# Merged products of k and b with a, and a state transpose in corners, in a chunked RWKV-7 kernel followed by a gated MLP

## The chip, the cores and the metric

The kernel runs on one core of a Trainium2 chip. A core has a matrix engine (PE, whose loading of stationary operands is shown apart as PEld), a vector engine (DVE), a scalar engine (ACT), a general engine (POOL) and a queue engine (SP) that issues transfers. Each has its own queue and works through it in order; semaphores tie them together. The metric is the device time of one execution in microseconds.

## The reference

Two stages follow each other. The first is a recurrence over 768 time steps for 4 batches of 8 heads with 40 channels; the second is a small MLP with the gate h * cos(h).

```python
for t in range(S):                       # S = 768, B = 4, H = 8, D = 40
    y[:, :, t] = einsum('bhd,bhde->bhe', rt, state)
    Sa = einsum('bhde,bhe->bhd', state, at)
    state = state * wt[:, :, None, :] - einsum('bhd,bhe->bhde', Sa, bt)
    state = state + einsum('bhd,bhe->bhde', vt, kt)
x = y.transpose(0, 2, 1, 3).reshape(3072, 320)
h = x @ w_in                             # 320 x 2048
out = (h * cos(h)) @ w_out               # 2048 x 320
```

All inputs and outputs are float32.

## The kernel before

**Chunks.** Time is cut into 24 chunks of C = 32 steps. Within a chunk the recurrence is written with matrices: strictly lower triangular 32 x 32 matrices of a with b (`nt`) and of a with k (`ag`), the inverse of one plus the first, and products with the state. The partition axis of 128 holds four blocks of 32, one for each batch (`blk`), or two halves of 64 of which 40 are used, one for each head parity e (`half`). Everything is float32, and one product of `mm` (L101) appears in the trace as two MATMULs and two LDWEIGHTS. A small product occupies only the part of the 128 x 128 array that its operands' partitions name: rows from where the stationary operand lies, columns from where the output lies. This text calls such a part a position.

**The steps of one chunk.** They are functions that issue to all engines:

- `p1_w`, `p1_a`, `p1_b`, `p1_n` prepare two chunks at a time. Running products of w are transposed, 1/w is taken (L395), b/w goes to `bn_b` (L396, on POOL), a times the products of w is kept transposed as `aT`, and `p1_b` transposes b/w to `bT`. `p1_n` multiplies bT with aT: 32 products of 32 stationary columns for each chunk, which ACT copies to `nt` (L459).
- After the `p1_n` of the second pair of a group of four chunks, a list of 33 small steps (`inverse`) starts: one DVE transpose (L486), 31 pairs of DVE operations (L494, L498) and one more transpose (L502) that leaves the inverses as `rt` for the whole group. The steps of the list are handed out one for each step of the main order.
- `p2_v`, `p2_k`, `p2_g` turn v, r and k/w; `p2_g` makes 32 products of k with a and 32 of v with r in one PSUM tile named gram. DVE masks the first to `ag` (L637).
- `ch_t` turns the state, which lies in `qz`, by eight transposes of 104 x 104 (L655), copied by ACT (L659). `ch_q` multiplies r with the turned state. `ch_x` adds 32 products of `ag` with v and 32 of aT with the state. `ch_s` multiplies with the inverse `rt`. `ch_z` makes the change of the state and the output `yt`.

**The MLP** is cut into pieces: `first_a` and `first_b` make h for 512 hidden columns and 256 tokens, and `second` multiplies with w_out. In the trace these are ph and po. ACT and DVE compute the gate between them. The tokens go through DRAM once (`xd`, L776 to L788) to be regrouped as `xT`.

**The order** is written by hand. For each chunk c a list `segs` names the chunk's own steps and places M at which one piece of the MLP may stand; which list is used depends on c % 4. `later(n, f)` issues f after n more steps. A group's inverse must be out before `ch_s` of its first chunk: while it isn't, a piece with four inverse steps is put in, or an inverse step alone. PSUM tiles of the small stages come from `at`, a ring of two buffers of two banks. The order of a small stage and the next piece is also coupled: after a step marked `small`, `first_b` does its 64-row products first.

**Loads** of inputs are issued by SP (L152), four for each tensor and chunk, one for each batch. The weights are rounded early in the kernel in 20 portions (`rounded`), with scratch tiles `mant`, `expo` and `sign`.

Of the kernel before, what the change touches and what calls it, by code (L numbers as in the profile page):

```python
# [9 lines left out]
F32 = mybir.dt.float32  # L10
# [10 lines left out]
def kernel(  # L21
# [55 lines left out]
    full = [slice(DP * e, DP * e + DP) for e in range(2)]  # L77
    every = slice(0, P)

    const = ctx.enter_context(tc.tile_pool(name="const", bufs=1))  # L80
# [112 lines left out]

    su = kept("su", [P, HH, C], 1, 1.0)[0]
    for i in range(4):
        nc.gpsimd.affine_select(
            su[blk[i]], su[blk[i]], pattern=[[0, HH], [1, C]], compare_op=ALU.is_gt, fill=0.0,
            base=0, channel_multiplier=-1,
        )
# [20 lines left out]

    WID = 512
    first_done, second_done = [], []

    def rounded(m, dst, src, by, by_sb):
# [16 lines left out]
        def taken():  # L241
            hi = t["words"][:, :, 1]
            t["mant"] = sb2.tile([P, WID], I32, tag="mant", name="mant")
            t["expo"] = sb2.tile([P, WID], I32, tag="expo", name="expo")
            nc.vector.tensor_scalar(t["mant"], hi, 0xFFFFF, None, ALU.bitwise_and)  # L245
            nc.vector.tensor_scalar(
                t["expo"], hi, 20, 0x7FF, ALU.logical_shift_right, ALU.bitwise_and
            )
            nc.scalar.activation(t["expo"], t["expo"], ACTF.Relu, bias=to_bits, scale=2.0**23)
            t["sign"] = sb2.tile([P, WID], mybir.dt.bfloat16, tag="sign", name="sign")  # L250
            nc.scalar.activation(t["sign"], hi, ACTF.Sign)
# [141 lines left out]
    def over_w(c, wn):  # L393
        rw = ring.tile([P, H, D], F32, tag="rw", name="rw")
        nc.vector.reciprocal(rw, wn)  # L395
        nc.gpsimd.tensor_tensor(unpad(bn_b[c % 7]), unpad(nat["b", c]), rw, ALU.mult)  # L396
        G["rw", c] = rw

    def a_W(c, aps):
# [38 lines left out]
    def p1_n(c):  # L438
# [34 lines left out]
        elif c < 8:  # L473
            lower()
        if c % 4 == 2 and c > 2:
            inv_space()

# [114 lines left out]
    def p2_kn(c):  # L592
        nc.gpsimd.tensor_tensor(unpad(kn_b[c % 2]), nat["k", c], G["rw", c], ALU.mult)
        nc.gpsimd.tensor_copy(vvm[c % 2][:, :, C : C + D], nat["v", c])
        landed(c)
# [23 lines left out]
    def p2_g(c):  # L619
        kT, vT, aT, rT = G["kT"], G["vT"], G["aT", c], G["rT", c]  # L620
        ps = at("gram")
        for j in range(4):
            for bb in range(B):
                for e in range(2):
                    mm(
                        ps[blk[bb], e, j * C : (j + 1) * C], kT[half[e], j, blk[bb]],
                        aT[half[e], j, blk[bb]], j == 0,
                    )
        for j in range(4):
            for bb in range(B):  # L630
                for e in range(2):
                    mm(
                        ps[blk[bb], e, (4 + j) * C : (5 + j) * C], vT[half[e], j, blk[bb]],
                        rT[half[e], j, blk[bb]], False,
                    )
        ag = sb2.tile([P, H, C], F32, tag="ag", name="ag")
        nc.vector.tensor_tensor(  # L637
            ag.rearrange("p (e j) t -> p e (j t)", e=2), ps[:, :, : HH * C],
            su.rearrange("p j t -> p (j t)").unsqueeze(1).to_broadcast([P, 2, HH * C]), ALU.mult,
        )  # L640
        v1 = ps[:, :, HH * C : 2 * HH * C].rearrange("p e (j t) -> p e j t", t=C)
        nc.scalar.copy(pick(vvm[c % 2], 0, (HH * NV + N72, 2), (NV, HH), (1, C)), v1)
        nc.vector.tensor_tensor(
            pick(vvm[c % 2], N72, (HH * NV - N72, 2), (NV, HH), (1, C)), v1,
            su.unsqueeze(1).to_broadcast([P, 2, HH, C]), ALU.mult,
        )
        G["ag", c] = ag


    def ch_t(c):  # L650
        ps = at("sT")
        n = DP + D
        G["s"] = sb1.tile([P, 2 * B, n], F32, tag="s", name="s")
        for i in range(2 * B):
            nc.tensor.transpose(  # L655
                ps[:n, i // 4, (i % 4) * n : (i % 4 + 1) * n], qz[:n, i // 2, i % 2, C : C + n], ident[:n, :n]
            )
        for i in range(2):
            nc.scalar.copy(G["s"][:n, 4 * i : 4 * i + 4].rearrange("p i e -> p (i e)"), ps[:n, i, : 4 * n])  # L659

    def ch_q(c):
        ps = at("qps")
        for i in range(2 * B):
            for e in range(2):
                for f in range(2):
                    mm(
                        ps[half[e], f, i * C : (i + 1) * C], G["s"][half[f], i, half[e]],
                        G["rT", c][half[f], 2 * (i % 2) + e, blk[i // 2]], i == 0,
                    )
# [6 lines left out]
    def ch_x(c):  # L676
        ps = at("x0ps")
        for j in range(4):
            o = C * (j // 2)
            for bb in range(B):  # L680
                for e in range(2):
                    mm(
                        ps[blk[bb ^ e], e, j * N72 : (j + 1) * N72], G["ag", c][blk[bb], 4 * e + j, :],
                        vvm[c % 2][blk[bb], 2 * j + e, o : o + N72], j == 0,
                    )
        if c:
            for j in range(4):
                o = (NZ - N72) * (j // 2)
                for bb in range(B):
                    for e in range(2):  # L690
                        mm(
                            ps[blk[bb ^ e], e, j * N72 : (j + 1) * N72],
                            G["aT", c][half[e], j, blk[bb]], qz[half[e], bb, j % 2, o : o + N72], False,
# [6 lines left out]
    def ch_s(c):  # L700
        ps = at("sps")
        x0 = G["x0"]
        for j in range(4):
            for bb in range(B):
                for e in range(2):
                    g = bb ^ e
                    mm(
                        ps[blk[bb], e, j * N72 : (j + 1) * N72], G["rt", c][blk[g], 4 * e + j, :],
                        x0[e][blk[g], j * N72 : (j + 1) * N72], j == 0,
                    )  # L710
# [7 lines left out]
        for e in range(2):  # L718
            nc.vector.tensor_tensor(  # L719
                pick(sm[e], D, (2 * N72 - D, 2), (N72, 2), (1, C)),  # L720
                pick(ps[:, e], 0, (2 * N72 + D, 2), (N72, 2), (1, C)),
                su.rearrange("p (f m) t -> p f m t", f=2), ALU.mult,
            )
        G["sm"] = sm

    def ch_z(c):
# [10 lines left out]
        for s, n in ((0, kn_b[c % 2]), (1, bn_b[c % 7])):  # L737
            for j in range(4):
                o = C - C * (j // 2)
                for bb in range(B):  # L740
                    for e in range(2):
                        first = wide and not s
                        mm(
                            ps[bb // 2][(full if first else half)[e], bb % 2, j * N72 : (j + 1) * N72],
                            n[blk[bb], 2 * j + e, : DP if first else D],
                            sm[e][blk[bb], j, :] if s else vvm[c % 2][blk[bb], 2 * j + e, o : o + N72],
                            first and j == 0,
# [138 lines left out]
    def p1(c):  # L886


        def first_w():
            p1_w(c)  # L890
            if c == 4:
                later(1, lambda: load(6, "w"))

        def both_a():
            p1_a(c)
            if c == 4:
                later(1, lambda: load(7, "w"))
# [6 lines left out]

        return [first_w, both_a, lambda: p1_b(c), lambda: p1_n(c)]

# [7 lines left out]
    def p2(c):  # L914
# [4 lines left out]

        return [lambda: p2_v(c), lambda: p2_k(c), last]  # L920

# [8 lines left out]
    with tc.manual_schedule():  # L930
# [119 lines left out]
        for c in range(NCH):  # L1050
            t, q, x, s, z = main(c)
            v, k, g = p2(c + 1) if c + 1 < NCH else [lambda: None] * 3
            q0 = c - c % 4 + 4
            fill, pn, pn4 = (1, 4), None, None
            if c == 0:
# [27 lines left out]
            elif c == 5:  # L1083
                pw, pa = p1(10)[:2]
                pb, pn = p8
                segs = [t, M, pb, q, M, pn, k, M, x, M, s, S6, M, z, M, S7, M, pw, v, M, g, pa, M]
            elif c % 4 == 0 and q0 < NCH:
                pb, pn = p1(q0)[2:]
                segs = [t, v, M, q, M, k, x, M, g, M, s, pb, M, z, M, pn, M, M]
                if q0 + 4 < NCH:  # L1090
                    segs.insert(-1, lambda: scanned(c // 4 + 2))
            elif c % 4 == 1 and q0 < NCH:
                pw, pa = p1(q0 + 2)[:2]
                segs = [t, M, pw, q, M, x, k, M, s, v, M, z, M, pa, M, g, M, M]
            elif c % 4 == 2 and q0 < NCH:
                pb, pn = p1(q0 + 2)[2:]
                segs = [t, M, pb, q, M, pn, v, M, x, M, s, k, M, g, M, z, M, M]
            elif c % 4 == 3 and q0 + 4 < NCH:
                pw, pa = p1(q0 + 4)[:2]
                segs = [t, M, pw, q, M, x, k, M, s, v, M, z, M, pa, M, g, M, M]  # L1100
            else:
                segs = [t, v, M, q, M, x, k, M, g, M, s, M, M, z, M, M]
            n = len(segs)
# [9 lines left out]
            for i, seg in enumerate(segs):  # L1113
# [8 lines left out]
                if seg is not M:  # L1122
                    G["kind"] = "q" if seg is q and c > 3 else "other"
                    step(seg, *((0, 0) if c < 3 and seg in (*firsts, *seconds) else fill), small=seg in (q, x, g, s, z, pn, pn4, *firsts, *seconds))
                    if seg not in (*firsts, *seconds) and (c < 2 or c == 2 and not done):
# [7 lines left out]
                while i == n - 1 and c > 3 and done < goal and c != 4 and allowed(c):  # L1133
                    piece(*fill)
                if seg is pn and (c == 3 or c > 4 and c % 4 == 2):
                    inv_steps.extend(by_blocks(q0) if c == 3 else inverse(q0))
        for g, work, j, _ in pieces[done:]:
# [35 lines left out]
```

## Time and profile before

| what | value |
|---|---|
| median of 3 runs | 800.21 us (799.5 to 800.78) |
| the profiled execution's own time | 800.58 us |
| its span, first to last instruction | 798.9 us |
| granted PE clock, mean over the span | 0.983; 1.00 in every stretch of 10 us from 100 to 790 us |
| POOL busy | 25% of the span |
| chain that ended last: largest parts | ph 22%, po 20%, x0ps 3%, dps 3%, gram 3%, rw (1/w) 3% |
| DMA queues of the inputs | 52.11 MB, 30.6% of 16 engines' span |

The chain of work that ended last is followed back from the last instruction; a share is the part of the span for which an engine or a line was what everything else waited for. A line of the timeline gives the start in us, the length in us, the engine, the source line, output and inputs, their shapes (rows times columns of the array for PE) and how many instructions were merged. In the table of groups the number ahead of the comma is the group's busy time in us, and the one behind it the mean length of one instruction in ns.

A period of four chunks takes 116 us in the middle of the kernel (387 to 503 us). DVE's busiest stretch in it is the one of the inverse.

### The profile page before, as it was taken

The page shows a single profiled execution, that of the slowest core. Times are in us where ns is not written, and L with a number is a line of the kernel's source. Part 1 is how long each engine was busy: PE and PEld are TensorE (multiplying, and loading weights), DVE is VectorE, ACT ScalarE, POOL GpSimd, SP SyncE. Part 2 cuts the span into 40 slices and gives each one's busy share as a digit, 9 for nine tenths or more (in the row PEclk, how much of TensorE's full clock was granted, in tenths as well). Part 3 has the DMA queues.
Part 4 walks back from the last instruction along what each step waited for, and adds up shares of the span by engine and source line. Part 5 has one row for each costly group of instructions (what it writes and reads, how often), then busy time and mean ns, then how long its engine had stood idle before and what let it go on. Part 6 is the DMA issues. An engine that isn't in the chain of part 4 may idle for free.

```text
span 798.9 us, 39602 instructions
## 1 busy us (share of the span) xinstructions
PE 745.9 (93%) x17812; PEld 571.0 (71%) x17812; DVE 486.7 (61%) x1025; ACT 383.4 (48%) x723; POOL 199.9 (25%) x354
## 2 busy tenths in 40 slices
PE   4768798999999999999999999999999999999997
PEld 4535576777766777777777787777787777777775
DVE  8768858864734896554895645994346863323331
ACT  1336567564435436545535635534545445354352
POOL 5326635230321330330330230332031122201000
PEclk9888899999999999999999999999999999999999
DMA  8575563343353314334214324223220222001000
GB/s 112 150 187 140 146 152 88 60 124 64 59 122 64 67 36 65 72 99 70 60 38 66 93 43 73 46 49 68 43 46 21 46 46 55 19 18 32 20 17 16
DMA packets 183304, 55.79 MB, mean 70 GB/s; under 512 B 157152, under 2 KB 178656, under 8 KB 183136
## 3 DMA queue, kind: packets, MB, share of 16 engines
q1 hardware_dynamic: 177440, 52.11, 30.6%
q8 instruction: 140, 2.29, 1.2%
q10 hardware_dynamic: 5440, 0.82, 0.8%
q0 software_dynamic: 256, 0.33, 0.3%
q14 instruction: 28, 0.23, 0.1%
HBM read 42.07 MB, written 11.14 MB: 67 GB/s over the span
## 4 chain that ended last, share of the span: by engine, by line
PE 65%; DVE 14%; DMA 5%; ACT 5%; issue 4%; POOL 3%; SPq 2%; DVEq 0%; ACTq 0%; POOLq 0%
PE ph L101 22%; PE po L101 20%; PE x0ps L101 3%; PE dps L101 3%; PE gram L101 3%; DVE rw L395 3%; PE vT L330 2%; PE sps L101 2%; PE qps L101 2%; PE nps L101 2%; DVE inv_tmp L494 2%; DVE inv L498 2%; DVE mant L245 1%; SPq L152 1%; PE kT L330 1%
## 5 line engine op out<-in xcount | busy, mean ns | idle before, releaser
L101 PE MATMUL po<-w_out_sb,gT 128*128 128x320 f32 x768 | 223.5, 439 | 0.1
L101 PE MATMUL ph<-xT,w_in_sb 128*128 128x256 f32 x768 | 185.7, 386 | 0.1
L101 PEld LDWEIGHTS po<-w_out_sb,gT 128*128 128x128 f32 x768 | 140.2, 190 | 54.6 <-issue 2.3
L101 PEld LDWEIGHTS ph<-xT,w_in_sb 128*128 128x128 f32 x768 | 139.3, 190 | 29.7 <-issue 12.4
L830 ACT ACTIVATE turns<-ph,rnd 128x512 f32<-128x512 f32 x96 | 64.1, 685 | 156.3 <-PE ph L101 155.9
L832 DVE SCALAR_TENSOR_TENSOR turns<-turns,ph 128x512 f32<-128x512 f32 x96 | 64.0, 683 | 109.4 <-ACT turns L830 109.2
L840 DVE TENSOR_TENSOR gT<-ph,turns 128x512 f32<-128x512 f32 x96 | 65.8, 686 | 38.4 <-ACT turns L837 38.4
L756 POOL TENSOR_TENSOR qz<-qz,wc 128x160 f32<-128x160 f32 x92 | 41.9, 475 | 168.5 <-DVE qz L755 167.9
L837 ACT ACTIVATE turns<-turns,half_pi 128x512 f32<-128x512 f32 x96 | 69.3, 722 | 3.1
L836 ACT ACTIVATE turns<-turns 128x512 f32<-128x512 f32 x96 | 60.1, 626 | 19.0 <-DVE turns L832 19.0
L101 PE MATMUL ph<-xT,w_in_tail 64*128 64x256 f32 (+1 forms) x512 | 54.6, 394 | 1.6 <-issue 1.6
L498 DVE TENSOR_TENSOR inv<-inv,inv_tmp 128x31 f32<-128x31 f32 (+15 forms) x124 | 51.2, 413 | 4.3
L755 DVE TENSOR_TENSOR qz<-dps,qz 128x160 f32<-128x160 f32 x92 | 28.9, 314 | 37.6 <-PE dps L101 37.3
L586 POOL COPY vp<-nat_v 128x320 f32<-128x320 f32 x24 | 11.7, 487 | 159.9 <-DMA nat_v<-in_v_dram 139.6
L494 DVE TENSOR_TENSOR inv_tmp<-u,inv 128x31 f32<-128x31 f32 (+15 forms) x124 | 48.5, 391 | 2.3
L395 DVE RECIPROCAL rw<-nat_w 128x320 f32<-128x320 f32 x20 | 42.8, 2142 | 0.1
L101 PEld LDWEIGHTS ph<-xT,w_in_tail 64*128 64x128 f32 (+1 forms) x512 | 32.2, 160 | 10.8 <-issue 7.3
L767 POOL TENSOR_TENSOR yt<-yt,wb 128x512 f32<-128x512 f32 x24 | 31.6, 1318 | 22.1 <-DVE yt L762 22.1
L659 ACT COPY s<-sT 104x416 f32<-104x416 f32 x46 | 20.8, 503 | 33.1 <-PE sT L655 33.1
L719 DVE TENSOR_TENSOR sm<-sps,su 128x128 f32<-128x128 f32 x48 | 11.7, 285 | 33.1 <-ACT sm L714 30.3
L396 POOL TENSOR_TENSOR bn<-nat_b,rw 128x320 f32<-128x320 f32 x22 | 19.9, 905 | 44.3 <-DVE rw L395 44.2
L671 ACT COPY qz<-qps 40x512 f32<-40x512 f32 x46 | 26.6, 579 | 6.8 <-PE qps L101 6.4
(136 smaller groups left out, 1100.3 us busy)
## 6 DMA issues: line engine op xcount, KB each, us to landing
words<-in_moe_w_in_dram SPq DMA_DIRECT2D x8, 512.0 KB
xd<-yt SPq DMA_DIRECT2D x48, 80.0 KB
out_dram<-ot SPq DMA_DIRECT2D x24, 160.0 KB
nat_k<-in_k_dram SPq DMA_DIRECT2D x92, 40.0 KB
nat_v<-in_v_dram SPq DMA_DIRECT2D x92, 40.0 KB
nat_r<-in_r_dram SPq DMA_DIRECT2D x92, 40.0 KB
nat_a<-in_a_dram SPq DMA_DIRECT2D x84, 40.0 KB
ws<-in_w_dram SPq DMA_DIRECT2D x5, 640.0 KB
```

What stands on the lines that cost most here:

```text
L101: nc.tensor.matmul(o, lhsT=lhsT, rhs=rhs, start=start, stop=stop, skip_group_check=True)
L395: nc.vector.reciprocal(rw, wn)
L494: nc.vector.tensor_tensor(tmp, u[:, j : j + 1, :j].to_broadcast([P, C - j, j]), x[:, j:, j : j + 1].to_broadcast([P, C - j, j]), ALU.mult,)
L498: nc.vector.tensor_tensor(x[:, j:, :j], x[:, j:, :j], tmp, ALU.subtract)
L755: nc.vector.tensor_tensor(z, pick(dp, 0, (2 * N72 + C, 2), (N72, 2), (1, D)), z, ALU.add)
L756: nc.gpsimd.tensor_tensor(z, z, wc.rearrange("p (f m b) -> p f m b", f=2, m=2)[:, :, :, bb] .unsqueeze(3).to_broadcast([P, 2, 2, D]), ALU. ...
L767: nc.gpsimd.tensor_tensor(yt.rearrange("p j b t -> p (j b) t"), yt.rearrange("p j b t -> p (j b) t"), wx, ALU.mult)
L830: nc.scalar.activation(n, u, ACTF.Identity, bias=rnd, scale=1.0)
L832: nc.vector.scalar_tensor_tensor(n, n, -ROUND, u, ALU.add, ALU.subtract)
L836: nc.scalar.activation(n, n, ACTF.Abs)
L837: nc.scalar.activation(n, n, ACTF.Sin, bias=half_pi, scale=-2.0 * math.pi)
L840: nc.vector.tensor_tensor(gT[:, 2 * e : 2 * e + 2].rearrange("p f t -> p (f t)"), us[e], ns[e], ALU.mult)
```

## The change

From chunk QT = 8 on, k/w is also loaded and divided early (`early_k`, `early_kn`), turned together with b/w (`p1_kb`), and interleaved so that each product has 64 stationary columns, 32 of k and 32 of b. `p1_kn` multiplies these with aT: 32 products a chunk give both triangular matrices. Its output has k and b on alternating blocks, so the copies to `nt` (ACT) and the masks to `ag` (DVE) are made for each block of 32 partitions. For the result to meet its partner, the odd heads of bn, kn, v and k/w are stored with their two halves of the partition axis exchanged (`placed`: three POOL operations instead of one), and `spot` gives the block in which a product finds its operands. `p2_k` is left out from there on, and `p2_g` keeps only the products of v and r. From chunk 6 on `ch_t` turns the state by 32 products of 40 x 40 with the identity. Scratch for the weights' rounding and the new tiles share one buffer, `cv`. The lists of steps are rewritten to hold `p1_kb` and `p1_kn` of each chunk, and the inverse starts behind the fourth `p1_kn` of a group.

```diff
+    QT = 8
+
+    def spot(c, bb, e):
+        p = bb ^ 2 * e
+        return (p, p ^ 1) if c >= QT else (bb, bb ^ e)
...
+    cv = const.tile([P, 5 * WID], F32, tag="cv", name="cv")
+    kb = cv[:, : 4 * P * 2]
+    ke = cv[:, 1024:1344].rearrange("p (h d) -> p h d", d=D)
+    kne = cv[:, 1344:1856].rearrange("p (h d) -> p h d", d=DP)
...
+    def placed(c, dst, x, by=None):
+        lo, hi = slice(0, P // 2), slice(P // 2, P)
+        parts = [(every, every, slice(0, H, 2)), (lo, hi, slice(1, H, 2)), (hi, lo, slice(1, H, 2))]
+        for to, of, h in parts if c >= QT else [(every, every, slice(0, H))]:
+            if by is None:
+                nc.gpsimd.tensor_copy(dst[to, h], x[of, h])
+            else:
+                nc.gpsimd.tensor_tensor(dst[to, h], x[of, h], by[of, h], ALU.mult)
...
+    def p1_kb(c):
+        ps = at("kbT")
+        turned(ps[:, 0], kne)
+        turned(ps[:, 1], bn_b[c % 7])
+        for i, o, n in ((0, 0, 3 * C), (1, C, C)):
+            nc.scalar.copy(
+                pick(kb, o, (4 * C, 2 * B), (n, 2), (1, C)),
+                pick(ps[:, i], 0, (2 * C, 2 * B), (C, 2), (1, C)),
+            )
...
+    def p1_kn(c):
+        ps = at("nps")
+        for j in range(4):
+            for x in range(2):
+                for m in range(2):
+                    for e in range(2):
+                        p = 2 * m + x
+                        bb = p ^ 2 * e
+                        mm(
+                            ps[slice(m * DP, (m + 1) * DP), e, (4 * x + j) * C : (4 * x + j + 1) * C],
+                            pick(kb[half[e]], (j * B + p) * DP, (1, DP)), G["aT", c][half[e], j, blk[bb]],
+                            j == 0 and x == 0,
+                        )
...
+        for g in range(B):
+            for x, to, put in (
+                (1 - g % 2, G["nt"][blk[g], :, c % 4].rearrange("p t e j -> p e j t"), nc.scalar.copy),
+                (g % 2, ag[blk[g]].rearrange("p (e j) t -> p e j t", e=2), None),
+            ):
...
     def ch_t(c):
         ps = at("sT")
+        if c > 5:
+            s = sb1.tile([P, 2, 2 * B, D], F32, tag="s", name="s")
+            for i in range(2 * B):
+                for e in range(2):
+                    for f in range(2):
+                        o = C + DP * f
+                        mm(
+                            ps[half[f], e, i * D : (i + 1) * D], qz[half[e], i // 2, i % 2, o : o + D],
+                            ident[half[e], half[e]], i == 0,
+                        )
...
     def ch_x(c):
                 for e in range(2):
+                    p, g = spot(c, bb, e)
                     mm(
-                        ps[blk[bb ^ e], e, j * N72 : (j + 1) * N72], G["ag", c][blk[bb], 4 * e + j, :],
-                        vvm[c % 2][blk[bb], 2 * j + e, o : o + N72], j == 0,
+                        ps[blk[g], e, j * N72 : (j + 1) * N72], G["ag", c][blk[p], 4 * e + j, :],
+                        vvm[c % 2][blk[p], 2 * j + e, o : o + N72], j == 0,
                     )
...
     def ch_s(c):
                 for e in range(2):
-                    g = bb ^ e
+                    p, g = spot(c, bb, e)
                     mm(
-                        ps[blk[bb], e, j * N72 : (j + 1) * N72], G["rt", c][blk[g], 4 * e + j, :],
+                        ps[blk[p], e, j * N72 : (j + 1) * N72], G["rt", c][blk[g], 4 * e + j, :],
                         x0[e][blk[g], j * N72 : (j + 1) * N72], j == 0,
                     )
...
             elif c % 4 == 2 and q0 < NCH:
-                pb, pn = p1(q0 + 2)[2:]
-                segs = [t, M, pb, q, M, pn, v, M, x, M, s, k, M, g, M, z, M, M]
+                kb2, kn2, kb3, kn3 = p1(q0 + 2)[2:]
+                segs = [t, M, kb2, q, M, kn2, v, M, x, kb3, M, s, M, kn3, M, z, M, g, M]
...
-                if seg is pn and (c == 3 or c > 4 and c % 4 == 2):
-                    inv_steps.extend(by_blocks(q0) if c == 3 else inverse(q0))
+                if seg is pn and c == 3:
+                    inv_steps.extend(by_blocks(q0))
+                if c > 4 and c % 4 == 2 and kns and seg is kns[1]:
+                    inv_steps.extend(inverse(q0))
```

## The prediction

> **What bounds the kernel now.** I read the page first (busy shares, then the chain that ended last), then PE's timeline over one steady period of four chunks (420 to 536 us), then DVE's over the same stretch. The page:
>
> ```profile
> PE 745.9 (93%) x17812; PEld 571.0 (71%) x17812; DVE 486.7 (61%) x1025; ACT 383.4 (48%) x723; POOL 199.9 (25%) x354
> ...
> PE 65%; DVE 14%; DMA 5%; ACT 5%; issue 4%; POOL 3%; SPq 2%; DVEq 0%; ACTq 0%; POOLq 0%
> ```
>
> PE is busy for 93% of the span, and from chunk 8 on its timeline has almost no holes. So an edit is worth the PE time that it adds or takes. A PE stage's price is the distance from its start to the next stage's start, not its summed busy time, since small products overlap. Timeline lines (start in us, length, work):
>
> ```profile
> 182.00 0.73 PE L101 MATMUL below<-rn,noff 32*32 32x16 f32 x64
> 182.66 2.42 PE L101 MATMUL po<-w_out_sb,gT 128*128 128x320 f32 x8
> ```
> ```profile
> 421.34 0.82 PE L101 MATMUL qps<-rT,s 40*40 40x32 f32 x64
> 421.98 1.14 PE L101 MATMUL ph<-xT,w_in_tail 64*64 64x256 f32 x16
> ...
> 429.39 0.73 PE L101 MATMUL gram<-aT,kT 40*32 40x32 f32 x62
> ...
> 429.95 0.73 PE L101 MATMUL gram<-rT,vT 40*32 40x32 f32 x62
> 430.61 2.42 PE L101 MATMUL po<-w_out_sb,gT 128*128 128x320 f32 x8
> ...
> 441.05 1.29 PE L101 MATMUL nps<-aT,bT 40*32 40x32 f32 x128
> 442.27 4.57 PE L101 MATMUL po<-w_out_sb,gT 128*128 128x320 f32 x16
> 446.68 0.88 PE L655 MATMUL sT<-ident,qz 104*104 104x104 f32 x8
> 447.40 1.91 PE L101 MATMUL ph<-xT,w_in_sb 128*128 128x256 f32 x8
> ...
> 458.05 0.88 PE L101 MATMUL sps<-x,rt 32*32 32x72 f32 x64
> 458.86 0.66 PE L330 MATMUL vT<-ident,vp 128*128 128x128 f32 x4
> ```
>
> Each fp32 product is two MATMULs (32 products, x64). The reader should see that 64 MATMULs cost 0.5 to 0.8 us whatever they compute. What sets that is in the single start times. sps starts in waves of 8, 62.5 ns apart (458.183, 458.246, 458.308); gram in waves of 8 about 32 ns apart; qps in waves of 4, 38 ns apart; below in waves of 4, 32 ns apart. The code gives the number of different positions (rows of the array x columns) that each stage uses: 8, 8, 4, 4. So one MATMUL runs at each position at a time, and a wave lasts as long as the longer of two things: streaming (72 columns: 62.5 ns, 0.87 ns a column) and loading the stationary operand (below streams 16 columns, 14 ns, yet needs 32 ns for 32 stationary columns; qps needs 38 for 40). After the first 33 or so, eight-position stages pause for 65 ns and run on at 8.3 ns a MATMUL, another limit, which leaves sps at 0.66 us from first start to last.
>
> ```profile
> L101 PEld LDWEIGHTS sps<-x,rt 32*32 32x32 f32 x1536 | 17.7, 106 | 13.8 <-issue 7.5 <-DVE x L697 3.9 <-DVE gT L840 1.3
> ...
> L101 PEld LDWEIGHTS dps<-vvm,kn 32*64 32x64 f32 x1280 | 16.2, 130 | 8.8 <-issue 6.5 <-DVE turns L832 1.3 <-ACT half L556 0.5
> ```
>
> A load of 64 columns is 24 ns longer than one of 32 (106 against 130 ns in the mean column; inside the waves 105 and 131, 26 apart). So a 64-column load needs 32 + 26 = 58 ns of its position.
>
> **The change, part by part.** Around a stage of small positions PE also loses 0.09 us going in (the last po before sps is followed after 0.363 us, before sT after 0.269) and, to the next full-size stage, 0.12 us after a 32-column stream, 0.15 after 72.
>
> 1. Products of k and b with a (16 chunks, 8 to 23). Out, for four chunks: the four pairs of gram stages, 4 x (0.09 + 0.53 + 0.69) = 5.24; kT's transposes, 0.44 to 0.49 each, 1.91; nps twice, 2 x (0.09 + 1.22) = 2.62; bT twice, 0.93 and 0.87, 1.80. Together 11.57 us. In: gram with v and r alone, 4 x (0.09 + 0.56 + 0.12) = 3.08; eight transposes a chunk for k and b, 0.93 each but 0.87 ahead of qps, 3.66; 32 products a chunk of 64 stationary columns at 4 positions, 16 waves of 58 ns, first to last start 15 x 58 + 20 = 0.89, so 4 x (0.09 + 0.89 + 0.12) = 4.40. Together 11.14. A gain of 0.43 us in four chunks, 1.7 in sixteen. Halving the MATMULs here halves no time, since half the positions carry loads nearly twice as long. Bounds of the gain: 0.3 us if 64 columns load in twice the 32 ns of 32, and 6.1 us at qps's 0.62 from first to last start.
>
> 2. Positions of x0ps and sps. To make the merged output fit, `spot` sends block p = bb ^ 2e to p ^ 1 for both e. The ag products of x0ps and all of sps then use four positions (0 to 1, 1 to 0, 2 to 3, 3 to 2) instead of eight. At 62.5 ns a wave of four, 16 waves: 15 x 62.5 + 20 = 0.96 us against 0.66. That is 0.30 us, twice a chunk, 16 chunks: +9.5 us. Bounds: 0 (the positions do not bind) to 72 ns a wave as qps's surplus of 11 ns over its 27 ns stream would give, +14. dps, gram and the aT half of x0ps keep eight positions. I take 9.5; the sps row is the same product.
>
> 3. State turned by 32 products (18 chunks, 6 to 23). sT costs 0.715 now (446.68 to 447.40) as full-size work without the losses around it. As 64 MATMULs of 40 stationary and 40 moving columns at 4 positions it is qps: 0.09 + 0.62 + 0.12 = 0.83. +0.12 x 18 = +2.1 us; bounds 0 and +4 (a 72-column sps's 0.81 plus its 0.09).
>
> 4. The inverse. It begins when the last n-product of its four chunks is out. Before, that is nps early in the chunk with c % 4 = 2 (481.93); now it is the fourth product, behind s (490.31) and another piece: 10 to 12 us later. DVE's rows and its reader:
>
> ```profile
> 486.76 1.23 DVE L486 STREAM_TRANSPOSE u<-nt 128x1024 f32<-128x1024 f32 x1
> ...
> 538.28 1.97 DVE L502 STREAM_TRANSPOSE rt<-inv 128x1024 f32<-128x1024 f32 x1
> ```
> ```profile
> 548.92 1.23 PE L101 MATMUL sps<-x,rt 32*32 32x72 f32 x64
> ```
>
> rt is ready at 540.25, 8.7 us ahead of its reader, so the delay eats the margin and a little more. At one step per PE step, 31 of the 33 inverse steps come before s; the kernel then puts one more piece ahead of it (1.8 us of PE work, no loss by itself). DVE's rows between u and rt sum to about 49 us (inverse 28, the rest 21), and PE's stages from the same point to that s, at the prices above, to about 50: DVE finishes as PE arrives. I charge 0.5 us at each of four places (q0 = 8, 12, 16, 20), +2.0. Bounds: -4 (the present waits of PE in this stretch, 0.67, 0.38 and 0.76 us, go) to +16.
>
> 5. Hidden work. ACT: four nt copies of 32 partitions a chunk in place of one of 128 (two of those take 1.03 us in a row), +1.5 us a chunk, and longer s copies, +0.3: about 31 us on 383. DVE: four masks of 0.42 for one, +20 on 487. POOL: bn, kn and vvm in three parts each and k/w a second time, three rows near 0.475 (qz's 160 columns) for one of 0.905: about 2.7 us a chunk, +43 on 200. All three stay below 65%, behind pieces of 1.8 to 4.5 us; uncovered, one late copy per chunk of 0.3 us would be 5 us. SP issues 64 more loads of k, four in 1.9 to 3.1 us. Its queue passes xd and nat loads behind them; it is idle for 5 to 7 us at the end of each long burst (323 to 328), which two such groups just fill, and xT is first read about half a chunk later. The weights' rounding, whose buffers k now reuses, ends at 140 us, before the first such load. I charge nothing.
>
> Sum: +9.5 + 2.1 - 1.7 + 2.0 = +11.9 us on the profiled execution's 800.58 (span 798.9), which is 0.4 above the median of the runs (800.21). Rounded down for that: 812.
>
> **The rivals.** *Number of instructions decides* (faster). PE's stages cost by count, not position: 64 columns at qps's rate give 6.1, sps and x0ps stay, sT costs gram's 0.78, +1.2. 800.6 - 6.1 + 1.2 = 795.7. For it: all 64-MATMUL stages lie between 0.5 and 0.8 us. Against it: waves of four where four positions are used, and 32 ns for a 16-column stream. [...]
>
> *Row groups decide.* The new order walks all four row blocks in turn, where now each comes twice running. If only a row's being taken held a product up, part 2 would cost nothing: 800.6 + 2.1 - 1.7 + 2.0 = 803.0. Against it: sps has 8 in a wave on four row blocks, below 4 on the same four. [...]
>
> *DVE becomes the bound at the inverse* (slower still). If rt comes 4 us late at each of four places, 812 + 14 = 826. For it: DVE is 92 to 97% busy from 500 to 540; against it: the sum above, with the small steps last.
>
> **How the numbers follow.** The forecast has 0.60 and its own range 806 to 820 (parts 2 and 4); the late inverse 0.13 (820 to 832); row groups, or half of part 2, 0.11 (799 to 806); instruction count 0.16 (790 to 799). The range 798 to 826 leaves out most of the last and the top of the second, 0.2 together. A measurement here tells 0.2%, 1.6 us, from no change: faster 0.17, same 0.06, slower 0.77.
>
> **What would show it.** sps and the first half of x0ps at about 1.11 and 1.08 us to the next start instead of 0.81; the 64-column stage at 1.0; sT at 0.75 or more; PE holes ahead of sps at chunks 8, 12, 16, 20 below 1 us. I am wrong if sps still takes 0.81, if the merged stage takes qps's 0.64, or if PE shows new holes behind ACT, POOL or SP.

## The result, and the profile after

The change costs time: 875.1 us (872.0 to 878.4, 4 runs) beside 800.5 us for the kernel before in the same comparison, a ratio of 1.092 with a 95% interval of 1.088 to 1.095. The prediction had the sign, 812 us in place of 875, and a range that ends at 826.

The page of the kernel after the change, busy time and share by engine, then the granted PE clock in 40 slices of the span, then the chain that ended last:

```profile
span 872.2 us, 39911 instructions
...
PE 780.4 (89%) x17780; PEld 592.2 (68%) x17780; DVE 507.4 (58%) x1073; ACT 426.2 (49%) x771; POOL 256.7 (29%) x499
...
PEclk9778999999987999999999997999999999999999
...
PE 58%; DVE 15%; ACT 10%; DMA 7%; issue 4%; SPq 4%; POOL 3%; POOLq 0%; DVEq 0%; ACTq 0%
```

Three things grew. The span is 73.3 us longer (872.2 against 798.9). PE idles for 91.8 us of it (872.2 less 780.4) where it idled for 53.0: 38.8 us. The mean granted clock is 0.956 in place of 0.983; 1 - 0.956 of 872.2 is 38.4 us, against 13.6: 24.8 us. What is left is 9.7 us, and that is the only part that the prediction summed up (9.5 + 2.1 - 1.7 = 9.9). That the two agree so closely is partly luck. The split belongs to these two executions: the mean clock was 0.949 to 0.956 in the four runs of the kernel after the change and 0.966 to 0.981 in 30 runs of the kernel before beside the experiments, and by the middle of both the loss of clock is nearer 20 us than 25. In the chain, ACT's share went from 5% to 10%.

The timeline of PE in the new kernel, about one end of a chunk with c % 4 = 1 and the start of the next (start, length, work; the idle time ahead of a line and what ended it stand in brackets):

```profile
516.43 1.14 PE L107 MATMUL nps<-aT,cv 40*64 40x32 f32 x64
517.49 2.42 PE L107 MATMUL po<-w_out_sb,gT 128*128 128x320 f32 x8
519.85 0.76 PE L107 MATMUL gram<-rT,vT 40*32 40x32 f32 x64
523.03 1.30 PE L107 MATMUL sT<-ident,qz 40*40 40x40 f32 x64 [2.43 <-DVE ag L550]
524.26 3.78 PE L107 MATMUL ph<-xT,w_in_sb 128*128 128x256 f32 x8
...
534.32 0.66 PE L344 MATMUL vT<-ident,vp 128*128 128x128 f32 x4
...
539.67 2.06 PE L107 MATMUL x0ps<-vvm,cv 32*32 32x72 f32 x64 [2.10 <-DVE cv L550]
```

The merged product (nps) takes 1.06 us to the next start, close to the 1.01 of the prediction (0.89 and 0.12). But the turn of the state, which needs nothing of it, starts 2.43 us late behind the last mask of that product, and the eight MATMULs of ph behind it take 3.78 us where they take 1.99 elsewhere. At 539.67 the same again. Holes of 0.3 us or more behind the masks add up to about 26 us from 200 us on.

Why the masks hold up a stage that does not read them is seen in the same kernel's timelines of ACT and of DVE, four entries each for one merged product:

```profile
535.29 0.57 ACT L548 COPY nt<-nps 32x256 f32<-32x256 f32 x1
536.34 0.59 ACT L548 COPY nt<-nps 32x256 f32<-32x256 f32 x1 [0.48 <-DVE cv L550]
537.42 0.58 ACT L548 COPY nt<-nps 32x256 f32<-32x256 f32 x1 [0.48 <-DVE cv L550]
538.48 0.58 ACT L548 COPY nt<-nps 32x256 f32<-32x256 f32 x1 [0.49 <-DVE cv L550]
```
```profile
535.90 0.41 DVE L550 TENSOR_TENSOR cv<-nps,su 32x256 f32<-32x256 f32 x1 [1.07 <-ACT nt L548]
536.97 0.42 DVE L550 TENSOR_TENSOR cv<-nps,su 32x256 f32<-32x256 f32 x1 [0.66 <-ACT nt L548]
538.03 0.42 DVE L550 TENSOR_TENSOR cv<-nps,su 32x256 f32<-32x256 f32 x1 [0.64 <-ACT nt L548]
539.09 0.43 DVE L550 TENSOR_TENSOR cv<-nps,su 32x256 f32<-32x256 f32 x1 [0.64 <-ACT nt L548]
```

Eight operations on one PSUM tile, each waiting for the one before on the other engine, from 535.29 to 539.52: 4.2 us. The tile is one of the two buffers of `at`. The stage after next that asks for a buffer (here x0ps; vT took the other) starts at 539.67, 0.15 us behind the last mask. In all 16 of these tiles of this kernel each of the eight but the first starts 0.03 us behind the end of the one before (three times 1.01 us, where DVE had other work), also where a mask and the next copy read different blocks. Why operations on different blocks wait for each other is not shown by these traces.

### The profile page after: what moved, and what is told of

Same layout as the page of the kernel before. It is cut to its first block, busy times and chain, and to the rows that moved or that the text cites. A ratio compares the mean times of both kernels' runs of the same rounds, so it can differ in the third digit from the quotient of the medians.

```text
span 872.2 us, 39911 instructions
## 1 busy us (share of the span) xinstructions
PE 780.4 (89%) x17780; PEld 592.2 (68%) x17780; DVE 507.4 (58%) x1073; ACT 426.2 (49%) x771; POOL 256.7 (29%) x499
## 4 chain that ended last, share of the span: by engine, by line
PE 58%; DVE 15%; ACT 10%; DMA 7%; issue 4%; SPq 4%; POOL 3%; POOLq 0%; DVEq 0%; ACTq 0%
PE ph L107 20%; PE po L107 17%; PE x0ps L107 4%; PE dps L107 4%; ACT nt L548 3%; PE sps L107 3%; SPq L158 3%; PE kbT L344 2%; DVE rw L409 2%; PE vT L344 2%; PE qps L107 2%; ACT turns L944 1%; DVE cv L550 1%; PE sT L107 1%; PE nps L107 1%
## 5 line engine op out<-in xcount | busy, mean ns | idle before, releaser
L107 PE MATMUL po<-w_out_sb,gT 128*128 128x320 f32 x768 | 231.1, 448 | 0.0
L107 PE MATMUL ph<-xT,w_in_sb 128*128 128x256 f32 x768 | 191.0, 394 | 0.5 <-DMA xT<-xd 0.5
L107 PEld LDWEIGHTS po<-w_out_sb,gT 128*128 128x128 f32 x768 | 142.4, 194 | 55.5 <-issue 5.2
L107 PEld LDWEIGHTS ph<-xT,w_in_sb 128*128 128x128 f32 x768 | 142.6, 194 | 32.9 <-issue 12.3
L548 ACT COPY nt<-nps 32x256 f32<-32x256 f32 x64 | 37.6, 587 | 42.5 <-PE nps L107 16.4
L570 DVE TENSOR_TENSOR inv_tmp<-u,inv 128x31 f32<-128x31 f32 (+15 forms) x124 | 51.5, 415 | 1.9
L421 POOL TENSOR_TENSOR bn<-nat_b,rw 64x160 f32<-64x160 f32 (+2 forms) x54 | 31.4, 582 | 39.5 <-DVE rw L409 24.9
L409 DVE RECIPROCAL rw<-nat_w 128x320 f32<-128x320 f32 x20 | 42.8, 2142 | 0.0
L107 PEld LDWEIGHTS ph<-xT,w_in_tail 64*128 64x128 f32 (+1 forms) x496 | 32.3, 168 | 10.2 <-issue 6.7
L107 PEld LDWEIGHTS sps<-x,rt 32*32 32x32 f32 x1536 | 23.5, 109 | 18.1 <-issue 14.2
```

The costliest lines, as they stand in the source:

```text
L107: nc.tensor.matmul(o, lhsT=lhsT, rhs=rhs, start=start, stop=stop, skip_group_check=True)
L548: put(to, of)
L570: nc.vector.tensor_tensor(tmp, u[:, j : j + 1, :j].to_broadcast([P, C - j, j]), x[:, j:, j : j + 1].to_broadcast([P, C - j, j]), ALU.mult,)
```

## The experiments

Times in the text are medians of the runs; the last table is made from the profiled executions. The kernel before, run beside each set of experiments, had medians of 798.2 to 802.2 us, so a difference of some 4 us between kernels of different sets shows little.

**Is it the eight evacuations?** One ACT copy and one DVE mask for the whole tile; with this layout every other block then gets the other matrix.

```diff
-        for g in range(B):
-            for x, to, put in (...
+        nc.scalar.copy(G["nt"][:, :, c % 4].rearrange("p t e j -> p e j t"), of(1))
+        nc.vector.tensor_tensor(ag.rearrange("p (e j) t -> p e j t", e=2), of(0), ...)
```

> The eight evacuations behind each merged product (4 of ScalarE, 4 masks of VectorE, 4.3 us in series) become one of each over 128x256; every other row block of the stationary and of the mask output then holds the other half, so the values differ, the work on every other engine is the same. Theory (the series of eight holds one of the two PSUM buffers and makes the holes, and the holes lower the clock): the 26 us of PE holes behind the masks go, and with them about two thirds of the 25 us of lost clock: 825 to 840 us, mean granted clock 0.97 or more, no hole of 2 us behind the masks. Rival 1 (the loads and GpSimd's pieces of k in chunks 5 to 7 set the pace): 865 or more. Rival 2 (TensorE's own small products cost more than their rows show): 860 or more with no holes left.

836.5 us (835.1 to 837.9), 38.6 less. No hole is left behind the masks, and the idle time of PE falls from 91.8 to 66.0 us. Both rivals would have kept it at 860 or above. The clock only rose to 0.964, where 0.97 was expected; two low stretches stayed at 210 to 265 us, behind the holes ahead of kbT.

**The buffer, or the work?** ACT copies the whole tile to SBUF first, and the eight operations read that.

```diff
+        st = cv[:, :512].rearrange("p (e n) -> p e n", e=2)
+        nc.scalar.copy(st, ps[:, :, : 2 * HH * C])
```

> ScalarE first copies the whole PSUM result to SBUF (128x512, 0.6 us), and the four copies and four masks read that, with the same outputs as before. Work on ScalarE grows by 16 times 0.6 us, VectorE's stays. Theory (it is the PSUM buffer that is held too long): nearly all of the relief of the single pass, 828 to 845 us. Rival (it is the work of ScalarE and VectorE that is too much, whatever it holds): 870 to 890.

847.0 us (843.4 to 850.6): 28 us back with more work on ACT than before, a little above the range. In ACT's timeline of this kernel the operations no longer take turns:

```profile
394.06 0.57 ACT L542 COPY cv<-nps 128x512 f32<-128x512 f32 x1
394.66 2.57 ACT L548 COPY nt<-cv 32x256 f32<-32x256 f32 x4
```

The buffer is free after 0.57 us, and the four copies run in one piece. So most of the loss is the buffer held for 4.2 us. The other 10 us are the difference to one_pass, which has less work on both engines; part of them is seen on PE, where kbT waits for 1.35 us three times (398, 520 and 643 us) until ACT, behind its four copies, has read the turned v and r out of the other buffer. No run gives the ring a third buffer.

**The turns, or their sum?** All four copies first, then the four masks.

> The kernel after the change, with the four ScalarE copies of each merged product ahead of its four VectorE masks, where they alternated (same outputs). Theory (the sum of eight operations in series is what counts, 4 times 0.58 and 4 times 0.42 us, and seven handoffs of about 0.06 us are only a tenth of it): 866 to 876 us. Rival (the alternation is the cost): 845 to 860.

870.8 us (870.2 to 871.3). The copies run for 2.4 us, then the masks for 1.7: 4.1 us in place of 4.2, and the holes ahead of x0ps are 1.9 to 2.0 us in place of 2.1. Ahead of the turn the hole is 1.35 us in place of 2.4: there 1.2 us of DVE's work on the gate stood between the first copy and its mask and lengthened the series to 5.25 us, and with the copies first it runs beside them. PE's idle time falls by 4 us (91.8 to 87.5), the clock is no better (0.954). So it is mostly the sum that counts, and the alternation is the smaller part.

**The holes at 211 and 264 us.** In the kernel after the change, on PE:

```profile
257.25 1.99 PE L107 MATMUL ph<-xT,w_in_sb 128*128 128x256 f32 x8
264.05 1.11 PE L344 MATMUL kbT<-ident,cv 128*128 128x128 f32 x4 [4.80 <-POOL cv L421]
```

The queue of SP stood for up to 11.9 us at the load of the early k (L504), whose one buffer POOL had not read yet. First attempt: two buffers for it.

```diff
-    ke = cv[:, 1024:1344].rearrange("p (h d) -> p h d", d=D)
+    kes = [cv[:, o : o + H * D].rearrange("p (h d) -> p h d", d=D) for o in (1024, 2368)]
```

> The early k has two buffers in place of one, so that its load no longer waits for GpSimd to have read the last one. Theory: the two holes of 4.6 and 4.8 us ahead of the k and b transposes at 211 and 264 us go or shrink, and some of the low clock behind them: 858 to 868 us. Rival 1 (the masks alone count, and the loads queue behind others anyway): 871 to 877. Rival 2 (this chain is the main cause): below 850.

869.7 us (868.9 to 870.4), some 5 us less, between the ranges of the theory and of rival 1; the two holes of 4.55 and 4.80 us stood unchanged. So the buffer was not what kbT waited for there. POOL's timeline of the kernel after the change says what was:

```profile
250.28 1.69 POOL L421 TENSOR_TENSOR bn<-nat_b,rw 128x160 f32<-128x160 f32 x3 [1.18 <-DVE rw L409]
259.74 1.69 POOL L421 TENSOR_TENSOR bn<-nat_b,rw 128x160 f32<-128x160 f32 x3 [7.76 <-issue]
261.49 0.45 POOL L662 COPY vp<-nat_v 128x320 f32<-128x320 f32 x1
261.88 0.46 POOL L662 COPY rp<-nat_r 128x320 f32<-128x320 f32 x1
262.30 1.70 POOL L421 TENSOR_TENSOR cv<-cv,rw 128x160 f32<-128x160 f32 x3
```

The last line is the early k of chunk 10, which needs only the 1/w of the first line's chunk. It stands behind b/w of chunk 11, which waits for a reciprocal on DVE (L409, 257.47 to 259.61 us), and behind vp and rp; POOL is idle for 7.76 us with its work queued in the wrong order. So the early k is issued ahead of the next chunk's w and b:

```diff
         def both_a():
+            if c >= QT:
+                early_kn(c)
             p1_a(c)
-            if c >= QT:
-                later(1, lambda: early_kn(c))
```

> The single pass of the run before (one ScalarE copy and one VectorE mask per merged product, values differ), and GpSimd's three pieces of the early k of chunk c are issued ahead of the work on chunk c+1's w and b, where they stood behind it. Theory (the two holes of 4.6 and 4.8 us ahead of the k and b transposes come from GpSimd's order: the early k stands behind the products of b and 1/w of the next chunk, which wait for VectorE's reciprocal): the 9.4 us of holes and the low clock of 200 to 280 us go: 815 to 826 us. Rival (the load of k is what is late, the order is not): the holes stay, 832 to 840.

838.9 us (838.5 to 839.3): nothing gained over one_pass. Both holes ahead of kbT are gone, but five of 1.5 to 3.1 us came ahead of ph, four of them behind a transfer. So the order made the two holes, as the theory has it, and the time is still the rival's. SP's queue and PE of this kernel:

```profile
483.99 0.37 SPq L881 DMA_DIRECT2D xd<-yt  x1
488.22 1.80 SPq L504 DMA_DIRECT2D cv<-in_k_dram  x4
490.12 0.39 SPq L891 DMA_DIRECT2D xT<-xd  x1
```
```profile
494.09 3.75 PE L107 MATMUL ph<-xT,w_in_sb 128*128 128x256 f32 x8 [3.07 <-DMA xT<-xd]
```

The load of the early k now stands between the store and the read-back of x and holds SP for 4 us until POOL has read its one buffer. The staged form with the same edit shows it too:

> The staged copy (same outputs) with GpSimd's early k issued ahead in the same way. Theory: 847 less the same 11 to 20 us, 826 to 836 us, some 10 us above the single pass, which is ScalarE's extra copies and the eight small operations. Rival (ScalarE's queue is the bound in this form): 840 or more.

846.6 us (845.9 to 847.2), no gain over 847.0. With the new order it is the second buffer that was missing:

> Single pass, early k ahead on GpSimd, and two buffers for the early k (values differ by the single pass). Theory (in the run before, the load of the early k stood in SP's queue between the store and the read-back of x, waiting up to 4 us for GpSimd to have read its one buffer, and made the four new holes of 2 to 3 us ahead of the first MoE product): these holes and the low clock behind them go, 9.8 plus some 7 us: 817 to 826 us, so that the early work on k and b costs little beyond TensorE's own longer stages (10 us) and the late inverse (5 us and its clock). Rival (the time goes elsewhere each time a hole is closed, because the whole of ACT, DVE, GpSimd and SP is too full): 832 or more.

827.1 us (825.8 to 828.5), 1 us above the range: 9.4 less than one_pass. Of the holes ahead of ph one of 4.1 us is left. The staged form:

> Staged copy (same outputs), early k ahead, two buffers for the early k. Theory: the holes ahead of the first MoE product (5 us) and the low clock behind them go: 834 to 842 us. Rival (ScalarE's queue, 10 us more of copies than in the single pass, takes the gain): 844 to 850.

839.3 us (838.9 to 839.8), as expected, and the fastest form that computes all of the change: 1.045 of the time before (1.039 to 1.051), slower still.

**TensorE's own price, measured alone.** The kernel before with only the positions of x0ps and s changed (values differ):

```diff
-                        ps[blk[bb ^ e], e, j * N72 : (j + 1) * N72], G["ag", c][blk[bb], 4 * e + j, :],
-                        vvm[c % 2][blk[bb], 2 * j + e, o : o + N72], j == 0,
+                        ps[blk[g], e, j * N72 : (j + 1) * N72], G["ag", c][blk[p], 4 * e + j, :],
+                        vvm[c % 2][blk[p], 2 * j + e, o : o + N72], j == 0,
```

> The kernel before the change, with only the 32 products of ag in x0 and the 32 of s put on four array positions from chunk 8 on, as the change puts them (the operands are read from other row blocks, so the values differ). Theory: 16 chunks times twice 0.30 us, all on the path: 808 to 812 us, with s and the first half of x0 at 1.11 to 1.14 us each. Rival 1 (the row groups bound the stage, not the positions): 802 to 804. Rival 2 (the waits behind the longer stages add to it): above 814.

806.9 us, a ratio of 1.0092 (1.0056 to 1.0128) to the 798.2 us of the kernel before in this comparison: 4.5 to 10.2 us. The time is 1 us under the range, which was counted from 800 us, and above that of rival 1. PE's timeline of this kernel, against 0.81 to the next start in the kernel before:

```profile
460.24 1.20 PE L107 MATMUL sps<-x,rt 32*32 32x72 f32 x64
461.38 0.65 PE L336 MATMUL vT<-ident,vp 128*128 128x128 f32 x4
```

And the kernel before with only the turn by 32 small products:

> The kernel before the change, with only the turn of the state by 32 small products in corners from chunk 6 on (same outputs). Theory: 18 times 0.04 us on TensorE, and two ScalarE copies of 0.7 us in place of 0.46 us ahead of q, of which some 0.1 us a chunk is waited for: 1 to 4 us slower than before. Rival (the copies are waited for in full, 18 times 0.48): 8 us or more slower.

808.3 us, a ratio of 1.0067 (1.0037 to 1.0098): 3.0 to 7.9 us, more than expected. Its timeline of PE says where:

```profile
450.36 4.57 PE L101 MATMUL po<-w_out_sb,gT 128*128 128x320 f32 x16
454.87 0.83 PE L101 MATMUL sT<-ident,qz 40*40 40x40 f32 x64
455.62 1.99 PE L101 MATMUL ph<-xT,w_in_sb 128*128 128x256 f32 x8
457.45 1.04 PE L330 MATMUL wT<-ident,nat_w 128*128 128x128 f32 x8
```

Against the lines of the kernel before that the prediction shows: po to sT 4.51 us where it was 4.41 (446.68 less 442.27), sT to ph 0.75 for 0.72, and ph to the next full-size stage 1.83 us, where it took 1.75 behind the transposes. Together some 0.21 us, most of it in the two neighbours. Not every chunk is like this one: in chunks 8, 12 and 16, where transposes of v stand behind the turn, the same three distances add up to 0.01 us more, and over all 18 chunks they add up to 2.8 us, 2.4 of it in the neighbours. Where the rest of the 3.0 to 7.9 us lies stays open. In the kernel after the change the turn was undone:

> The state is turned by 8 transposes in every chunk again, as before the change; all else is as after. Theory: 18 times 0.04 us of TensorE and 18 times 0.5 us of ScalarE's copies, of which part is waited for: 868 to 874 us. Rival (the 32 products of the turn disturb TensorE's queue or the chain of the state beyond what their row shows): below 865.

872.2 us (870.9 to 873.6), 2.9 us less, which the spread of the kernel after the change (872.0 to 878.4) does not tell from nothing.

**Does the idle PE itself bring the low clock?** Dummy matmuls in the idle places of the kernel after the change, of chunks 6, 10, 14 and 18:

> The kernel after the change, with dummy matmuls (8 to 10 of 0.25 us, 5 ahead of the third place) put in TensorE's queue where it stood idle behind the masks in chunks 6, 10, 14 and 18: ahead of the turn of the state 2.4 us, ahead of the first x0 product 2.1 us, ahead of the last products 1.2 us. The waits stay as long, TensorE is only not idle in them. Theory (an idle stretch of some 2 us is followed by a lower granted clock, which costs about as much again): clock 0.97 or more and 857 to 868 us. Rival (the lower clock has another cause, or the dummies only take the place of the wait): 872 to 880.

885.0 us (884.2 to 885.7), 10 more. This did not test it: ahead of x0ps the dummies asked for a buffer of po and waited themselves (4.4 us in place of 2.1), and the ten ahead of the turn filled 1.0 of the 2.4 us. Again, with more of them and only where po's buffer is at hand:

```diff
+        FILL.update({(m, i): n for m in (10, 14, 18) for i, n in ((0, 24), (15, 12))})
```

> The kernel after the change, with 24 dummy matmuls (0.1 us each) ahead of the turn of the state and 12 ahead of the last products in chunks 10, 14 and 18, so that TensorE is not idle in the 2.4 and 1.2 us there; the waits of 2.1 us ahead of the first x0 product stay idle. Theory (the idle stretch brings the lower granted clock): no granted clock under 0.97 within 10 us behind the filled places (0.66 at 395 to 400 and 0.54 at 525 to 530 us in the kernel after), and 864 to 872 us. Rival (the waits alone and the low clock have a common cause elsewhere): the same low stretches at the same places, 873 to 878.

871.8 us (871.3 to 872.3). Stretches of 5 us of PE (from and to, length, busy time, granted clock, then the DMA share and GB/s, not used here), first of the kernel after the change, then of this one:

```profile
520.00:525.00 5.00, 2.57 (x130) 0.77 0.40 67
525.00:530.00 5.00, 5.00 (x51) 0.54 0.44 69
```
```profile
520.00:525.00 5.00, 4.66 (x157) 1.00 0.34 56
525.00:530.00 5.00, 5.00 (x99) 1.00 0.49 79
...
405.00:410.00 5.00, 3.17 (x16) 1.00 0.45 72
410.00:415.00 5.00, 4.72 (x138) 0.66 0.40 62
```

Behind all the filled places the clock stays at 1.00, also at the two (395 and 523 us) behind which it had dropped, and at 410 us it drops at an x0ps that was left idle. The turn waits as long behind gram in both kernels (3.18 us from start to start), so it is PE's idling that lowers the clock, not what made it wait. The 3.3 us that this saved are no more than the spread of the kernel after the change.

**The last 25 us.** The inverse came 3.9 us late ahead of chunk 20. Two of its steps were handed out at a time from chunk 19 on, in single_first_two:

```diff
-                segs = [t, v, M, q, M, x, M, g, M, s, M, M, z, M, M]
+                segs, fill = [t, v, M, q, M, x, M, g, M, s, M, M, z, M, M], (2, 4)
```

> Single pass, early k ahead, two buffers, and from chunk 19 on two steps of the inverse with each step of work in place of one (values differ by the single pass). Theory (the inverse of the last group came 3.9 us late because VectorE was given one step at a time and stood idle between): the hole ahead of s in chunk 20 and the low clock behind it go: 819 to 824 us. Rival (VectorE is full there and the steps only push other work back): 826 or more.

827.7 us (827.0 to 828.5): the hole is gone and nothing is gained. New ones came instead (1.0 us ahead of a turn, 1.7 us ahead of a q, behind ACT's copy of the turned state), and a low clock at 641 us, ahead of both. The same with the turn undone:

> As inverse_sooner, with the state turned by 8 transposes again. Theory (the turn costs what it cost in the kernel before, 3 to 8 us, once no hole hides it): 4 to 8 us under inverse_sooner, 812 to 818 us, and so within some 5 us of the kernel before plus the 9 us of four positions. Rival 1 (it costs the 2 to 3 us that undoing it brought in the kernel after): 817 to 822. Rival 2 (a further loss is still unnamed): 820 or more.

825.4 us (822.0 to 828.7), above both of the first two ranges and in that of rival 2, a loss still unnamed; the spread is too wide to price the turn again. What is left is seen by groups of chunks. The table is worked out from the starts of the stage sT in the profiles, in us:

| kernel | chunk 5 to 8 | 8 to 12 | 12 to 16 | 16 to 20 | 20 to end | idle PE | clock lost |
|---|---|---|---|---|---|---|---|
| before | 95.4 | 115.7 | 116.0 | 110.7 | 155.2 | 53.0 | 13.6 |
| after | 126.8 | 128.0 | 130.7 | 121.5 | 161.0 | 91.8 | 38.4 |
| one_pass | 109.3 | 121.0 | 120.2 | 115.9 | 160.7 | 66.0 | 30.1 |
| single_first_two | 100.5 | 120.5 | 120.0 | 115.0 | 161.0 | 59.1 | 23.1 |
| before_4pos | 94.1 | 117.7 | 118.2 | 112.9 | 157.7 | 48.3 | 20.2 |

Of the 73 us by which the span grew, 31 lie in chunks 5 to 8, where the masks and POOL's order meet, 11 to 15 in each of the next three groups and 6 in the last. Once those are undone (single_first_two), a group costs 4.0 to 4.8 us more than before. The four positions alone make 2.0 to 2.2 of it, and the rows of the turn, in the kernel before, 0.5 to 0.7. The small holes do not make the rest: single_first_two has 1.5 to 1.9 us of holes of 0.3 to 0.7 us in a group (0.66 ahead of the second half of x0ps, 0.43 ahead of s, 0.45 ahead of vT), and the kernel before has 1.5 and 1.8 us in other places in the first two of these groups (0.76 ahead of vT, 0.33 to 0.67 ahead of s, 0.38 ahead of the next vT), 0.8 in the third. So 1 to 2 us of a group stay without a cause. The clock column includes the first 100 us, where 13.7 to 18.8 us are lost in the kernels of the table, whatever the change.

## Why the prediction was wrong

- *Part 1, the merged products:* right as far as the rows go. The stage takes 1.06 us (1.01 predicted), kbT 0.93 and, ahead of qps, 0.97 (0.93 and 0.87), gram of v and r alone 0.69 (0.68 predicted: 0.56 between the first and the last start of gram's MATMULs in the kernel before, 429.92 to 430.49 us, and 0.12). The small gain of this part was not run alone.
- *Part 2, four positions:* right. 1.13 us to the next start for s and the first half of x0ps (1.11 and 1.08 predicted), and 4.5 to 10.2 us measured alone against 9.5. The rivals of instruction count and of row groups fall with it.
- *Part 3, the turn:* mis-sized, 2.1 us against 3.0 to 7.9. The term of 0.83 us (loss going in, stage, loss to the next) measured 0.85. What it left out is the stage behind, where ph is 0.08 us longer; but not all 18 chunks have these neighbours, and all in all the rows give 2.8. The upper bound of +4 is 3.3 by the part's own figures (0.90 less 0.715, 18 times).
- *Part 4, the inverse:* the delay was there, 0.43, 0.42, 0.44 and 3.71 us, 5.0 in all against 2.0, within its bounds. Closing the longest did not pay.
- *Part 5, the hidden work:* this is the step that failed, at "I charge nothing". It counted the busy time that the change adds to ACT, DVE and POOL and compared it with their shares (all below 65%, which still holds, though ACT grew by 43 us in place of 31 and POOL by 57 in place of 43). It did not ask what the eight evacuations hold while they run: one of two PSUM buffers for 4.2 us, sixteen times. It allowed 5 us for copies that come late; the single pass gave back 38.6. The queues were searched for room, not for what stands in front of what (the 5 to 7 us of SP's queue that were taken for room, at 323 to 328 us, are a wait of the store of x for POOL's yt): POOL's order of the early k and SP's wait for its buffer cost another 9.4.
- *The clock* had no place in the sum, since it was 1.00 nearly everywhere before. Some 20 to 25 of the 73 us are lost clock, nearly all of it behind holes.

What the prediction gave as a sign of its being wrong, new PE holes behind ACT, POOL or SP, is nearly what came: the largest part stands behind DVE's masks, which wait in turn for ACT's copies, the next behind POOL. No rival priced it, and the range did not hold it.

## What to carry to other kernels

When an edit splits one evacuation into several, price the time that the PSUM buffer stays taken, not the engines' busy time: count the operations in series on the tile, and name the stage that asks for the ring's next buffer. For each moved step, read what stands ahead of it in each queue (here the step on POOL that waits for the next chunk's 1/w, with 7.76 us idle, and the load of k on SP, with 4 us), because a queue with room still blocks. Where PE was never idle for 2 us (from 100 us on in the kernel before 1.61 us at most), the first holes of that length also cost clock, here half to two thirds as much again as the added idle time.

## What the runs showed of the hardware

Of the seven idle stretches of 2 us or more from 300 us on in the kernel after the change (2.1 to 3.7 us), four were followed by a lower clock: behind the one that ends at 523.03 us, ph took 3.78 us in place of 1.99, at a granted clock of 0.50. None of the stretches of 1.2 us or less was. Idle stretches of 2.1 and 2.4 us were enough in part of the cases: those that end at 394.98 (2.40 us), 523.03 (2.43) and 539.67 (2.10) were followed by half clock, those at 410.35 (2.10), 653.59 (2.42) and 667.11 (2.10) were not.

The traces also show in which cases. In every kernel here the granted clock is either 1.00 or 0.50, and its low stretches begin on one grid of 3.41 us in each kernel and last whole steps of it (3.41, 6.83, 10.24 or 13.65 us), but for one at the end of the span. What tells the cases apart is the idle time that falls into one step. Some steps of the kernel after the change (from and to, length, PE's busy time, granted clock, then the DMA share and GB/s, not used here):

```profile
519.33:522.75 3.42, 1.27 (x67) 1.00 0.25 42
522.75:526.16 3.41, 3.13 (x69) 0.50 0.46 76
526.16:529.57 3.41, 3.41 (x13) 0.50 0.49 74
529.57:532.99 3.42, 3.42 (x89) 1.00 0.47 75
```
```profile
406.69:410.10 3.41, 1.56 (x6) 1.00 0.41 63
410.10:413.52 3.42, 3.17 (x137) 1.00 0.55 88
```

The hole of 2.43 us ahead of the turn leaves PE idle for 2.15 us of one step, and the next two steps run at half clock. The hole of 2.10 us at 408 us is cut by the end of a step, 1.85 us on one side, and costs no clock. Over all the kernels here, from 100 us on, each of the 52 steps at full clock with 2.0 us or more of idle was followed by half clock, and of those with less than 1.25 us only two were; in between it was 33 of 83. In the kernel after the change alone it was 5 of 5, none of 198 and 4 of 8; the kernel before has no step of the first kind, and none of 201 and of 2. Both exceptions (at 641 us in inverse_sooner and 653 us in one_pass_first) follow a step that held 1.6 us of dummy products of a single column (pad, 60 of them), which the profile counts as busy (in inverse_sooner PE shows 5.00 us busy from 635 to 640 us and 4.98 from 640 to 645, at 0.66); behind the same 60 in the kernel after the change, at 688 us, the clock stayed at 1.00. So the same hole can cost clock or not, by where in the grid it falls, and that is luck.

In before_turn the stage of small products cost its neighbours too: the full-size stage behind the turn took 1.83 us where it took 1.75 behind transposes, and the one ahead 4.51 where it took 4.41. Over all 18 chunks the neighbours make 2.4 us, and in chunks 8, 12 and 16 next to nothing.
